# Blocks of 32 tokens in four column tiles, placed inside a big block's second layer

## The chip, the cores and the metric

The kernel runs on one core of a Trainium2 chip. The metric is the device time of that core, in microseconds (us). An execution has a span, from the first to the last instruction that the profile records, and a little time around it that counts too. TensorE multiplies matrices (PE in the profile, PEld for its loads of stationary operands), VectorE (DVE), ScalarE (ACT) and GpSimd (POOL) do the rest, and SyncE (SP) issues transfers.

## The reference: windowed attention, then one expert for each token

Eight sequences of 576 tokens go through attention of 8 heads with a causal window of 64 positions. The result, 4608 rows of 512 numbers, goes into a layer of eight experts:

```
fresh_e = argmax(logits[b, s])
e = fresh_e if s == 0 or local_gate[b, s] < 0.5 else prev_e
p = softmax(logits[b, s])
h = maximum(x[b, s] @ w1[e], 0.0)      # w1[e]: 512 x 1024
out[b, s] = p[e] * (h @ w2[e])         # w2[e]: 1024 x 512
```

So each token uses exactly one expert, and which one is known only after attention. Everything is float32. The numbers of tokens for the experts are uneven, so when an expert's tokens are gathered in blocks, the last of them leave a remainder.

## The kernel before, in words

**Stages.** Attention takes the first 137 us or so. The router (class `Router`) works out for every token its expert, its probability and its place in a list of blocks; `first` does so for the first tokens, `second` for all the rest, beside the first three expert blocks. The result are tables: `idx` (which token stands in which row of which slot of 128 rows), `pw` (its probability), `gx` (the row to gather) and `ej` (the expert of each block). The rest of the time goes to class `Experts`.

**Blocks.** An expert's tokens are cut into big blocks of 256 rows (two slots). A remainder of 65 to 192 takes a small block of 128 rows, one of up to 64 a half block, and more than 192 rounds up to a big block. Since the program is fixed and the numbers are not, `SURE` says how many blocks of each kind are always run: 13 big, 4 small, 4 half, after three big blocks that the first part of the tokens fills (`FB`). If an input needs more, a branch at the end (`more`) runs the others.

**A big block.** Both layers of most big blocks are written as a 2x2 multiplication with seven products in place of eight. The first layer is `big_hidden` (L1164): seven products of 16 records of 128 columns each (L1184), additions on VectorE (L1195) and relus on ScalarE (L1196). It needs sums and differences of quarters of x (`xs`) and w1 (`ws1`), which `prepare` (L1134) has VectorE compute; `big_hidden` itself has VectorE compute those of w2 (`ws2`, L1157) and of the hidden layer (`hs`, L1149). The second layer is `big_result` (L1216): seven products of 8 records of 256 columns each (L1227), copies scaled by the probability on ScalarE (L1232, L1252), three additions on VectorE (L1236), and a scatter of each slot's rows to the output on POOL (L1257). An f32 matmul of the program appears as two records in the profile.

**A half block.** `hidden` (L1275) puts a stationary of 64 columns of w1 into each of two column tiles of TensorE, so that 64 rows of x move through both at once: 64 matmuls, 128 records. `result` (L1294) keeps the hidden layer stationary and moves two halves of w2: 16 matmuls, 32 records. One copy on ScalarE (L1297) and one scatter by half rows (L1298, table `idxh`) follow. A small block uses the same functions with the whole array (L1275, L1307).

**Order.** `run` (L1326) makes a list of blocks. After the three first ones it takes big blocks 0 to 12; after each odd one a half or a small block stands, and one small and one half block come last. For every block in turn it calls `hidden`, then `turn` for the next block (L1123: transposes of the gathered rows on TensorE at L1129, a copy on VectorE at L1130, and `prepare` if the block is big), then `result`. So TensorE's order is hidden layer, transposes of the next block, second layer. From the third block on, the order on TensorE, VectorE and ScalarE is as written; before that only TensorE's is, and a scheduler places the rest.

**Loads.** Each block loads its expert's w1 and w2, 2 MB each, on SP's queue (L1116) into a ring of four buffers, two blocks ahead. A new load waits until the buffer that it takes is free. Rows of x are gathered by an indirect transfer on POOL (L1104). A scatter to the output waits for the landing of the scatter ahead of it.

Of the kernel before, what the change touches and what calls it, by code (L numbers as in the profile page):

```python
# [41 lines left out]
FB = 3  # L42
# [8 lines left out]
NBLK = NB + E + E  # L51
SURE = (LEFT + E * HF) // BIG - E // 2, E // 2, E // 2
# [27 lines left out]
def kernel(  # L80
# [25 lines left out]
                pwh=const.tile([P, E], F32, name="pwh"), idx1=const.tile([P, FIRST], U32, name="idx1"),  # L106
# [585 lines left out]
class Router:  # L692
# [217 lines left out]
    def experts_of(self, ej, n, ends):  # L910

        vec, tl = self.nc.vector, self.tl
        ec = tl("ec", 1, NBLK, E)
        b = 0
        for m, end in ends:
            vec.tensor_tensor(ec[:, b:b + m], self.iob[:, :m].to_broadcast([1, m, E]),
                              self.mid(end[0:1, :]).to_broadcast([1, m, E]), op=Alu.is_ge)
            b += m
        ef = tl("ef", 1, NBLK)
        vec.tensor_reduce(ef[:, :n], ec[:, :n], axis=AX.X, op=Alu.add)  # L920
        vec.tensor_scalar(ej, ef[:, :n], float(E - 1), None, Alu.min)
# [77 lines left out]
    def second(self, psum):  # L999
# [18 lines left out]
        ns = tl("ns", P, E)  # L1018
        self.shifted(ns, rest, HF - 1, P.bit_length() - 1)
        send = tl("send", P, E)  # L1020
        vec.tensor_tensor_scan(send, ns, self.zero[:, :E], 0.0, Alu.add, Alu.add)
        soff = tl("soff", P, E)
        vec.tensor_tensor(soff, send, ns, op=Alu.subtract)
# [3 lines left out]
        nh = tl("nh", P, E)  # L1027
        vec.tensor_tensor(nh, cnt, limh, op=Alu.is_gt)
        hend = tl("hend", P, E)
        vec.tensor_tensor_scan(hend, nh, self.zero[:, :E], 0.0, Alu.add, Alu.add)  # L1030
        hoff = tl("hoff", P, E)
        vec.tensor_tensor(hoff, hend, nh, op=Alu.subtract)
# [9 lines left out]
        vec.tensor_scalar(steph, steph, float(P), float((HF0 - SM0) * P), Alu.mult, Alu.add)  # L1042
        CE = [P, CV, E]
# [5 lines left out]
        yield 6.0, False  # L1049
        plh = tl("plh", *CE)  # L1050
        vec.tensor_tensor(plh, self.rank, mid(limh).to_broadcast(CE), op=Alu.is_ge)
        vec.tensor_tensor(plh, plh, mid(steph).to_broadcast(CE), op=Alu.mult)
        vec.tensor_tensor(pl, pl, plh, op=Alu.add)
# [5 lines left out]
        self.experts_of(ej[:, :NBLK], NBLK, [(NB, bend), (E, send), (E, hend)])  # L1059
        more = tl("more", 1, 1)  # L1060
        vec.tensor_scalar(more, hend[0:1, E - 1:], float(SURE[2]), None, Alu.is_gt)
        vec.scalar_tensor_tensor(more, send[0:1, E - 1:], float(SURE[1]), more, Alu.is_gt, Alu.max)
        vec.scalar_tensor_tensor(ej[:, NBLK:], bend[0:1, E - 1:], float(SURE[0]), more, Alu.is_gt, Alu.max)
        yield 6.0, False
        at = yield from self.table(psum, slice(0, CV), NS, lo, hi, tabs["idx"], tabs["pw"], tabs["gx"])

        for i in range(2):
            vec.tensor_scalar(tabs["idxh"][i * HF:(i + 1) * HF], at[:HF, HF0:], 2.0, float(i), Alu.mult, Alu.add)
            vec.tensor_copy(tabs["pwh"][i * HF:(i + 1) * HF], tabs["pw"][:HF, HF0:])

# [7 lines left out]
class Experts:  # L1078
# [12 lines left out]
    def rows(self, st, n):  # L1091
        tabs = self.tabs
        if n < 0:
            idx, pw, gx, rows = tabs["idx1"], tabs["pw1"], tabs["gx1"], ZR + 1
            slots = range(-2 - 2 * n, -2 * n)
        else:
            idx, pw, gx, rows = tabs["idx"], tabs["pw"], tabs["gx"], N + 2
            slots = range(2 * n, 2 * n + 2) if n < NB else range(SM0 + n - NB, SM0 + n - NB + 1)
        st.update(x=[], slots=slots, idx=idx, pw=pw, rows=P, big=len(slots) == 2, fast=len(slots) == 2 and n not in PLAIN)
        if n >= NB + E:  # L1100
            st.update(half=n - NB - E, rows=HF)
# [21 lines left out]
    def turn(self, st, quiet):  # L1123
        nc, n = self.nc, st["rows"]
        st["xt"] = xt = self.xtp.tile([P, DK, BIG], F32, name="xt")
        for i, x in enumerate(st["x"]):
            tp = self.ps_t.tile([P, DK, P], F32, name="tp")
            for kk in range(DK):
                nc.tensor.transpose(tp[:, kk, :n], x[:n, kk * P:(kk + 1) * P], self.ident[:n, :n])  # L1129
            (nc.scalar.copy if quiet else nc.vector.tensor_copy)(xt[:, :, i * P:i * P + n], tp[:, :, :n])  # L1130
        if st["fast"] and not quiet:
# [84 lines left out]
    def big_result(self, st):  # L1216

        nc = self.nc
        a, s, b, t = st["ha"], st["hs"], st["w2q"], st["w2t"]
# [19 lines left out]
        u = keep(0, px, pw[0])  # L1239
        product(py, s[0], t[0], stop=False)  # L1240
        z = keep(1, py, pw[1])
        product(px, s[1], t[1], False, False)
        v = keep(2, px, pw[0])
        product(pz, a[0][1], b[1][0])
        put(0, 0, pz, u)
        product(px, s[2], t[2], False, False)
        put(1, 1, px, z)
        product(py, s[3], b[1][1], False)
        put(0, 1, py, v)
        self.scatter(st, 0, y[0])  # L1250
        product(px, a[1][1], t[3], False)
        nc.scalar.activation(y[1][:, :w], px, Act.Copy, scale=pw[1])  # L1252
        self.scatter(st, 1, y[1])

# [29 lines left out]
    def result(self, st, step):  # L1284
        nc = self.nc
        if st["fast"]:
            return self.big_result(st)
# [38 lines left out]
    def run(self, ctx, rt, last=None):  # L1326
# [27 lines left out]
        small = list(range(NB, NB + SURE[1]))  # L1354
        half = list(range(NB + E, NB + E + SURE[2]))
        between = half[1:] + small
# [4 lines left out]
        order += between + half[:1]  # L1361
# [3 lines left out]
        for i, n in enumerate(order):  # L1365
# [11 lines left out]
            if i + 2 > FB and i + 2 < len(order):  # L1377
                jobs.append(self.fetch(order[i + 2]))
            self.hidden(jobs[i], quiet, step)
            if i + 1 < len(order):  # L1380
                self.turn(jobs[i + 1], i + 1 < FB)
            self.result(jobs[i], step)

    def more(self, ctx):

        self.space(ctx)
        for n in [*range(SURE[0], NB), *range(NB + SURE[1], NB + E), *range(NB + E + SURE[2], NBLK)]:
# [3 lines left out]
            self.result(st, lambda: None)  # L1391

# [48 lines left out]
```

## Time and profile before

| what | value |
|---|---|
| median of 3 runs | 658.93 us (657.99 to 662.63) |
| the profiled execution | 659.11 us, span 657.1 us |
| TensorE busy | 629.8 us, 96% |
| loads of stationary operands busy | 544.8 us, 83% |
| VectorE busy | 401.2 us, 61% |
| ScalarE, POOL busy | 181.8 us (28%), 125.8 us (19%) |
| records of half blocks: hidden / second layer | 512 of L1275 / 128 of L1294 |
| mean DMA rate | 252 GB/s |

A busy time is the union of an engine's recorded spans; a matmul's span includes its way through the pipeline, so the distance from one start to the next says more of its cost than its own duration. In a timeline a line gives the start (us from the beginning of the span), the duration of the merged group, engine, source line, operation, output and inputs, the tile of TensorE (rows x columns of the stationary operand, written 128*64), the moving shape, and the number of records; square brackets hold the idle time before it and what ended it. Idle time of an engine that is not the bottleneck costs nothing by itself.

### The profile page before, as it was taken

The page shows a single profiled execution, that of the slowest core. Times are in us where ns is not written, and L with a number is a line of the kernel's source. Part 1 is how long each engine was busy: PE and PEld are TensorE (multiplying, and loading weights), DVE is VectorE, ACT ScalarE, POOL GpSimd, SP SyncE. Part 2 cuts the span into 40 slices and gives each one's busy share as a digit, 9 for nine tenths or more (in the row PEclk, how much of TensorE's full clock was granted, in tenths as well). Part 3 has the DMA queues.
Part 4 walks back from the last instruction along what each step waited for, and adds up shares of the span by engine and source line. Part 5 has one row for each costly group of instructions (what it writes and reads, how often), then busy time and mean ns, then how long its engine had stood idle before and what let it go on. Part 6 is the DMA issues. An engine that isn't in the chain of part 4 may idle for free. (4 is left out here: it accounts for less than half of the span.)

```text
span 657.1 us, 14909 instructions
## 1 busy us (share of the span) xinstructions
PE 629.8 (96%) x6431; PEld 544.8 (83%) x6431; DVE 401.2 (61%) x723; ACT 181.8 (28%) x314; POOL 125.8 (19%) x131
## 2 busy tenths in 40 slices
PE   7888988899999999999999999999999999999995
PEld 7777767675757999889989998999799979997974
DVE  6675589665984866378628835852765276527310
ACT  4756655421111232112212121221122112211200
POOL 4322122220014111121104113211311130101011
PEclk9999998899999999999999999999999999999999
DMA  8999999895436555595578748746864685457540
GB/s 337 415 346 360 351 377 355 327 378 199 161 144 241 195 212 218 173 397 204 184 278 315 269 180 314 289 169 215 305 240 165 221 309 219 161 213 283 193 157 23
DMA packets 22032, 165.80 MB, mean 252 GB/s; under 512 B 3485, under 2 KB 4515, under 8 KB 11972
## 3 DMA queue, kind: packets, MB, share of 16 engines
q1 hardware_dynamic: 13108, 135.24, 55.4%
q0 software_dynamic: 8848, 29.50, 11.3%
q8 instruction: 53, 0.87, 0.5%
q14 instruction: 23, 0.19, 0.1%
HBM read 145.85 MB, written 19.40 MB: 251 GB/s over the span
## 5 line engine op out<-in xcount | busy, mean ns | idle before, releaser
L1257 POOL DMA_INDIRECT out_dram<-y,idx x36 | 40.9, 1136 | 335.6 <-DVE y L1236 149.2
L1184 PE MATMUL hp<-xs,ws 128*128 128x128 f32 x672 | 79.6, 275 | 0.0
L1184 PEld LDWEIGHTS hp<-xs,ws 128*128 128x128 f32 x672 | 77.3, 192 | 0.0
L1227 PE MATMUL hp<-ws,hs 128*128 128x256 f32 x336 | 77.1, 379 | 0.0
L1275 PE MATMUL hp<-xt,w 128*64 128x64 f32 (+2 forms) x896 | 74.1, 260 | 0.0
L1275 PEld LDWEIGHTS hp<-xt,w 128*64 128x64 f32 (+1 forms) x896 | 68.6, 161 | 5.8 <-issue 2.4
L1227 PEld LDWEIGHTS hp<-ws,hs 128*128 128x128 f32 x336 | 63.8, 190 | 8.7
L1195 DVE TENSOR_TENSOR h<-hp,keep 128x512 f32<-128x512 f32 x42 | 28.8, 690 | 57.3 <-PE hp L1184 57.3
L1104 POOL DMA_INDIRECT xg<-xs,gx x40 | 45.7, 1144 | 72.7 <-PE tp L1129 58.9
L1307 PE MATMUL yp<-w,h 128*128 128x512 f32 x128 | 56.4, 593 | 0.0
L1184 PEld LDWEIGHTS hp<-xt,w 128*128 128x128 f32 x448 | 53.0, 192 | 2.9 <-issue 1.9
L1184 PE MATMUL hp<-xt,w 128*128 128x128 f32 x448 | 54.9, 276 | 0.0
L1236 DVE SCALAR_TENSOR_TENSOR y<-hp,pw,kept 128x256 f32<-128x256 f32 x42 | 19.7, 480 | 57.1 <-issue 33.3
L1227 PE MATMUL hp<-w,h 128*128 128x256 f32 x224 | 53.3, 381 | 0.0
L416 DVE TENSOR_TENSOR p<-p,mask 128x1024 f32<-128x1024 f32 x31 | 38.6, 1244 | 20.6 <-ACT p L411 20.5
L380 PEld LDWEIGHTS sp<-w 64*64 64x64 f32 x1296 | 37.6, 134 | 16.3 <-issue 13.1
L411 ACT ACTIVATE p<-sp 128x512 f32<-128x512 f32 x72 | 39.3, 596 | 40.1 <-PE sp L380 37.9
L426 PE MATMUL xo<-va,p 128*64 128x74 f32 (+1 forms) x576 | 45.7, 233 | 3.3 <-DVE va L343 3.3
L426 PE MATMUL xo<-vb,p 128*64 128x74 f32 (+1 forms) x576 | 45.7, 233 | 3.2 <-ACT p L300 1.5
L380 PE MATMUL sp<-w 64*64 64x128 f32 (+1 forms) x1296 | 43.3, 265 | 5.5 <-issue 4.7
L426 PEld LDWEIGHTS xo<-vb,p 128*64 128x64 f32 x576 | 39.9, 141 | 7.9 <-issue 4.7
L1307 PEld LDWEIGHTS yp<-w,h 128*128 128x128 f32 x128 | 23.7, 190 | 26.9 <-issue 26.1
(257 smaller groups left out, 945.9 us busy)
## 6 DMA issues: line engine op xcount, KB each, us to landing
w<-in_w_dram SPq DMA_DIRECT2D x48, 2048.0 KB, 9.0
w<-in_kq_dram SPq DMA_DIRECT2D x17, 1024.0 KB, 9.4
xs<-x POOLq DMA_DIRECT2D x9, 1024.0 KB
va<-in_v_dram SPq DMA_DIRECT2D x5, 1184.0 KB
vtt<-in_vt_dram SPq DMA_DIRECT2D x5, 1024.0 KB
va<-in_v_dram SPq DMA_DIRECT2D x3, 1040.0 KB, 9.0
va<-in_v_dram SPq DMA_DIRECT2D x2, 520.0 KB, 6.6
w<-in_kq_dram SPq DMA_DIRECT2D x2, 512.0 KB
```

The costliest lines, as they stand in the source:

```text
L380: nc.tensor.matmul(sp[j][c * WIN:(c + 1) * WIN, a:b], lhsT=kt[h, hp, block * WIN:(block + 1) * WIN], rhs=qt[h, hp, a:b], start=not biased, ...
L411: nc.scalar.activation(p[:, j], sp[j], Act.Exp, scale=DH ** -0.5)
L416: masked.append(nc.vector.tensor_tensor(p, p, m.to_broadcast([P, 2, SC]), op=Alu.mult))
L426: nc.tensor.matmul(xo[par * WIN:(par + 1) * WIN, j, s * VW:s * VW + n], lhsT=p[:, j, b * WIN:(b + 1) * WIN], rhs=w[:, s, 2 * hp + j, :n], ...
L1104: self.nc.gpsimd.indirect_dma_start(out=x, out_offset=None, in_=self.xs[:rows, :], in_offset=bass.IndirectOffsetOnAxis(ap=gx[:, s:s + 1], ...
L1184: nc.tensor.matmul(out[:, m, :], lhsT=a[:, kk, m * P:(m + 1) * P], rhs=b[:, kk, :], start=start and m + kk == 0, stop=stop and (m, kk) == ...
L1195: nc.vector.tensor_tensor(o, x, y, op=add)
L1227: nc.tensor.matmul(out, lhsT=a[:, m, :], rhs=b[:, m, :], start=start and m == 0, stop=stop and m == FK // 2 - 1, skip_group_check=True)
L1236: nc.vector.scalar_tensor_tensor(y[i][:, j * w:(j + 1) * w], x, pw[i], y2, Alu.mult, Alu.add)
L1257: self.nc.gpsimd.indirect_dma_start(out=self.out[:, :], out_offset=bass.IndirectOffsetOnAxis(ap=st["idx"][:, s:s + 1], axis=0), in_=y, in_ ...
L1275: nc.tensor.matmul(hp[a, i, :], lhsT=st["w1"][:, kk, m * P:(m + 1) * P][:, a], rhs=st["xt"][:, kk, :n], start=(kk == 0), stop=(kk == DK - 1))
L1307: nc.tensor.matmul(yp, lhsT=st["h"][:, m, i * P:(i + 1) * P], rhs=st["w2"][:, m, :], start=(m == 0), stop=(m == FK - 1))
```

## The change

A fourth kind of block is added. A remainder is now rounded up to a multiple of 32 and written as 128, 64 and 32 (`count` in `second`): a remainder of up to 32 takes a *quarter* block, 33 to 64 a half, 65 to 96 a half and a quarter, 97 to 192 starts with a small one. Fixed numbers are 13 big, 4 small, 2 half, 2 quarter. A quarter shares a slot of 128 rows with a half of the same number: rows 0 to 63 are the half's, rows 64 to 95 the quarter's. Tables `idxq` and `pwq` serve its scatter by quarter rows.

A quarter's computation comes in three parts, `one`, `turned` and `two`. `one` keeps 32 rows of x stationary in each of four column tiles and moves a fourth of w1's columns through each; the hidden layer comes out with its rows as partitions, so `turned` transposes it; `two` keeps it stationary and moves fourths of w2. These parts are not a block of their own in the order: `big_result` of the big block ahead gets `hooks` and calls one after each of its products: `one` after the first, `turned` after the second, `two` after the third, nothing after the fourth, the transposes and copies of the following block's x after the fifth, its `prepare` after the sixth. Elsewhere the following block is turned and prepared before the second layer, as it was.

Quarters stand after big blocks 2 and 6; small blocks move up to stand after big blocks 1, 3, 5 and 7, one half after 9, and the other half block is last, behind big block 12. In `experts_of` the table of comparisons becomes bf16.

```diff
-NBLK = NB + E + E
-SURE = (LEFT + E * HF) // BIG - E // 2, E // 2, E // 2
+QR = P // 4
+KINDS = NB, NB + E, NB + 2 * E
+NBLK = KINDS[-1] + E
+SURE = (LEFT + E * HF) // BIG - E // 2, E // 2, E // 4, E // 4
...
-        ns = tl("ns", P, E)
-        self.shifted(ns, rest, HF - 1, P.bit_length() - 1)
-        send = tl("send", P, E)
-        vec.tensor_tensor_scan(send, ns, self.zero[:, :E], 0.0, Alu.add, Alu.add)
-        soff = tl("soff", P, E)
-        vec.tensor_tensor(soff, send, ns, op=Alu.subtract)
+        r = tl("r", P, E)
+        self.shifted(r, rest, QR - 1, QR.bit_length() - 1)
+
+        def count(name, x, many):
+
+            n = tl("n" + name, P, E)
+            vec.tensor_scalar(n, x, float(many), None, Alu.is_ge)
+            end = tl(name + "end", P, E)
+            vec.tensor_tensor_scan(end, n, self.zero[:, :E], 0.0, Alu.add, Alu.add)
+            off = tl(name + "off", P, E)
+            vec.tensor_tensor(off, end, n, op=Alu.subtract)
+            return n, end, off
+
+        ns, send, soff = count("s", r, 4)
+        vec.scalar_tensor_tensor(r, ns, -4.0, r, Alu.mult, Alu.add)
+        nh, hend, hoff = count("h", r, 2)
+        vec.scalar_tensor_tensor(r, nh, -2.0, r, Alu.mult, Alu.add)
+        _, qend, qoff = count("q", r, 1)
...
+        vec.tensor_tensor(plh, self.rank, mid(limq).to_broadcast(CE), op=Alu.is_ge)
+        vec.tensor_tensor(plh, plh, mid(stepq).to_broadcast(CE), op=Alu.mult)
+        vec.tensor_tensor(pl, pl, plh, op=Alu.add)
...
-    def turn(self, st, quiet):
+    def turn(self, st, quiet, later=False):
         nc, n = self.nc, st["rows"]
+        a = slice(HF, HF + n) if "quarter" in st else slice(n)
...
-        if st["fast"] and not quiet:
+        if st["fast"] and not quiet and not later:
             self.prepare(st)
...
         product(px, a[0][0], b[0][0], stop=False)
         u = keep(0, px, pw[0])
+        hook()
         product(py, s[0], t[0], stop=False)
         z = keep(1, py, pw[1])
+        hook()
...
+    def quarter(self, st):
+
+        nc, s = self.nc, st["quarter"]
+        w, n = F // 4, D // 4
+
+        def one():
+            yp = self.ps_y.tile([P, D], F32, name="yp")[:, :w]
+            for kk in range(DK):
+                for j in range(4):
+                    nc.tensor.matmul(yp[j * QR:(j + 1) * QR], lhsT=st["xt"][:, kk, :QR],
+                                     rhs=st["w1"][:, kk, j * w:(j + 1) * w], start=kk == 0, stop=kk == DK - 1)
+            st["hq"] = hq = self.one.tile([P, w], F32, name="qh")
+            nc.scalar.activation(hq, yp, Act.Relu)
+
+        def turned():
+            tp = self.ps_t.tile([P, DK, P], F32, name="tp")[:, :w // P]
+            for i in range(w // P):
+                nc.tensor.transpose(tp[:, i], st["hq"][:, i * P:(i + 1) * P], self.ident)
+            st["ht"] = ht = self.one.tile([P, w // P, P], F32, name="qt")
+            nc.scalar.copy(ht, tp)
+
+        def two():
+            yp = self.ps_y.tile([P, D], F32, name="yp")[:, :n]
+            for m in range(FK):
+                for j in range(4):
+                    k, i = divmod(m, w // P)
+                    nc.tensor.matmul(yp[j * QR:(j + 1) * QR], lhsT=st["ht"][:, i, k * QR:(k + 1) * QR],
+                                     rhs=st["w2"][:, m, j * n:(j + 1) * n], start=m == 0, stop=m == FK - 1)
+            y = self.one.tile([P, n], F32, name="qy")
+            nc.scalar.activation(y, yp, Act.Copy, scale=self.tabs["pwq"][:, s:s + 1])
+            nc.gpsimd.indirect_dma_start(
+                out=self.out.rearrange("n (i d) -> (n i) d", i=4),
+                out_offset=bass.IndirectOffsetOnAxis(ap=self.tabs["idxq"][:, s:s + 1], axis=0),
+                in_=y, in_offset=None, bounds_check=4 * N - 1, oob_is_err=False)
+
+        return one, turned, two
...
-        small = list(range(NB, NB + SURE[1]))
-        half = list(range(NB + E, NB + E + SURE[2]))
-        between = half[1:] + small
+        between = [*range(NB, NB + SURE[1]), *range(KINDS[1] + 1, KINDS[1] + SURE[2])]
+        quarters = list(range(KINDS[2], KINDS[2] + SURE[3]))
         for n in range(SURE[0]):
             order.append(n)
             if n % 2 and between:
                 order.append(between.pop(0))
-        order += between + half[:1]
+            elif n % 4 == 2 and quarters:
+                order.append(quarters.pop(0))
+        order += between
+        order.append(KINDS[1])
...
+            if n >= KINDS[2]:
+                continue
             self.hidden(jobs[i], quiet, step)
-            if i + 1 < len(order):
-                self.turn(jobs[i + 1], i + 1 < FB)
-            self.result(jobs[i], step)
+            if i + 1 == len(order):
+                self.result(jobs[i], step)
+                continue
+            self.turn(jobs[i + 1], i + 1 < FB)
+            hooks = ()
+            if order[i + 1] >= KINDS[2]:
+                one, turned, two = self.quarter(jobs[i + 1])
+                after = jobs[i + 2]
+                hooks = one, turned, two, (lambda: None), (lambda: self.turn(after, False, True)), \
+                    (lambda: self.prepare(after))
+            self.result(jobs[i], step, hooks)
```

## The prediction

> **What bounds the kernel now.** First the page: busy time of each engine, then the forty slices.
>
> ```profile
> PE 629.8 (96%) x6431; PEld 544.8 (83%) x6431; DVE 401.2 (61%) x723; ACT 181.8 (28%) x314; POOL 125.8 (19%) x131
> PE   7888988899999999999999999999999999999995
> ```
>
> From slice 8 (131 us) to the last, TensorE is full. So the expert stage is a queue of matmuls, and an edit there is worth the TensorE time it takes out, less any new gap. Next the timeline of TensorE over one big block (313.39), one half block (338.66) and the next big block (347.17).
>
> ```profile
> 313.39 1.95 PE L1184 MATMUL hp<-xt,w 128*128 128x128 f32 x16
> ...
> 325.99 0.46 PE L1129 MATMUL tp<-ident,xg 64*128 64x64 f32 x4
> 326.37 1.99 PE L1227 MATMUL hp<-w,h 128*128 128x256 f32 x8
> ...
> 338.66 3.95 PE L1275 MATMUL hp<-xt,w 128*64 128x64 f32 x128
> ...
> 343.56 3.67 PE L1294 MATMUL yp<-w,h 128*64 128x256 f32 x32
> 347.17 2.05 PE L1184 MATMUL hp<-xt,w 128*128 128x128 f32 x16
> ...
> 372.74 1.95 PE L1184 MATMUL hp<-xt,w 128*128 128x128 f32 x16
> ```
>
> Nothing idles between the groups. A big block followed by a big one lasts 372.74 - 347.17 = 25.57 us; big and half together last 347.17 - 313.39 = 33.78. A half block costs 33.78 - 25.57 = 8.21 us.
>
> Two more stretches of that timeline price packing: the gate's eight matmuls (L312, stationaries of 32 columns in four column tiles), and attention scores (L380) in tiles of 64x64.
>
> ```profile
> 108.84 1.06 PE L312 MATMUL r<-vtt,wg2s 128*32 128x512 f32 x8
> 109.84 1.12 PE L380 MATMUL sp<-w 64*64 64x128 f32 x36
> 110.89 0.66 PE L327 MATMUL r<-ident,gs 128*128 128x128 f32 x4
> ```
>
> Last, the timelines (start, duration, and in brackets the idle time before and its releaser) of VectorE and of the scatters on POOL.
>
> ```profile
> 183.70 0.42 DVE L1157 TENSOR_TENSOR xs<-xt 128x256 f32<-128x256 f32 x1 [3.18 <-ACT xt L1130]
> ...
> 285.21 0.43 DVE L1157 TENSOR_TENSOR xs<-xt 128x256 f32<-128x256 f32 x1
> ...
> 291.38 1.21 DVE L1157 TENSOR_TENSOR ws<-w 128x1024 f32<-128x1024 f32 x1
> ...
> 328.23 0.42 DVE L1130 COPY xt<-tp 128x256 f32<-128x256 f32 x1
> ```
>
> ```profile
> 627.10 0.98 POOL L1257 DMA_INDIRECT out_dram<-y,idx  x1 [21.65 <-DVE y L1236]
> 635.64 0.98 POOL L1257 DMA_INDIRECT out_dram<-y,idx  x1 [7.56 <-DMA out_dram<-y,idx]
> ...
> 651.08 0.98 POOL L1298 DMA_INDIRECT out_dram<-y,idxh  x1 [5.31 <-ACT y L1297]
> ```
>
> A big block's preparation takes VectorE 285.21 to 291.38 = 6.17 us; the sums of w2 then 4.67 (to 296.05), where the first relu addition follows at once: VectorE was behind there already.
>
> **What the Trainium skill says.** "TensorEngine Tiling (Array Packing)", Tiling Modes and Key Properties: 128x32 is four tiles that work in parallel, and changing the mode drains TensorE. The trace agrees: a 512-wide matmul on the whole array takes 7.03/16 = 0.43 us (L1307), so eight in four tiles would be 0.86, and they took 109.84 - 108.84 = 1.00; I read 0.14 as the drain, and L1294 shows as much (3.61 us against 32 x 0.108 = 3.46). "TensorE: Matmul & The Clock Gate", "Wait — 56ns, not 53.3ns?": matmuls never start closer than about 25 ns. Here L380 gives 1.05/36 = 29 ns with the drain, L1275 3.88/128 = 30. "DMA: Bandwidth & Descriptors", Issuing engines are not separate DMA queues: all queues share 16 engines. Agreed: the scatter of 627.10, beside a load of weights, lets the next go after 8.5 us.
>
> **The change part by part.**
>
> *Which blocks.* From the reference's router and the split rules I worked out each expert's leftover. Before: 13 big, 4 small, 4 half. After: 13, 4, 2 half, 2 quarter (leftovers of 9 and 18 tokens). All four counts equal what SURE provides for, so the rare path is not taken. Two half blocks become two quarters; jobs, loads of 4 MB and the 40 scatters stay in number.
>
> *Removed.* 2 x 8.21 = 16.42 us of TensorE.
>
> *Added on TensorE, for a quarter.* Counts are records: an f32 matmul appears as two in the trace. (a) Four transposes of x: the half's take 0.57 us with the switches (338.66 - 313.39 = 25.27 for the big block with them; 25.57 less the 0.87 of eight 128-wide ones = 24.70 without any); I take 0.5 (0.4 to 0.6). (b) `one`: 32 matmuls 256 wide; a whole-array one takes 1.73/8 = 0.216, in four tiles 32 x 0.216/4 = 1.73, with the drain 1.87. (c) `turned`: two transposes, 2 x 0.11 = 0.22, no change of mode. (d) `two`: 64 matmuls 128 wide; 7.14/64 = 0.112 each, over four 0.028, at the start-to-start floor; 64 x 0.028 = 1.79, at 30 ns 1.92; with the drain 2.0. Sum 4.6 us. Bounds: 4.2 with no drains; if only two of four tiles overlapped, (b) 3.5 and (d) 3.6, sum 7.8; not below 4.2, since the columns must stream.
>
> *Added waits on TensorE.* (e) `one` needs the quarter's xt, copied by VectorE after the four `hs` sums. At 328.23 that copy starts 1.86 us after the first product (326.37); I take 0.28 us for 128 elements (0.42 for 256, 0.68 for 512). So xt is ready near 2.2, and `one` could start at 1.8: 0.4 us of gap (0 to 0.5). The other six products queue behind it. (f) The next big block's `prepare` moves from ahead of the second layer's additions to behind the third one. Let T be the end of the sixth product. The addition starts 0.27 after its product and makes room after 0.43, at T + 0.7; prepare ends at T + 6.9; w2's sums at T + 11.5; two relu additions of 0.69 end at T + 12.9. TensorE runs product seven (1.73) and six first-layer products (1.787 each), and asks at T + 12.45 for the second of those additions, since the seventh product accumulates on what it reads. Gap 0.5 us (0 to 1.0). Queued behind it are the block's remaining products. The first sum of w1 comes at T + 3.4, wanted at T + 3.5: 0.1 more. So a quarter costs 4.6 + 0.4 + 0.5 + 0.1 = 5.6 us.
>
> *Hidden.* ScalarE's two copies and the scaling (0.47 us each by L1297's kind) lie under products of 1.73 us; without that cover up to 0.5 each. Weights: the following block's w1 is asked for when the second layer starts (R) and is wanted by VectorE near R + 17; its w2 takes the quarter's freed w1 slot near R + 4 and is wanted near R + 23. A load takes 8.5 us in the median, 10.3 at most: cover of 6 us or more; past it each microsecond is one of TensorE. On POOL the quarter's scatter stands ahead of two gathers and the big block's scatters; the gathers run two blocks ahead, and y buffers are wanted again 20 us later. On SP the order stays.
>
> *Router.* By the order in which the changed program's instructions stand, 15 more on VectorE before the table: three of 296 elements at 0.38 us cadence, 12 small ones at 0.1 to 0.2, some 2.3 to 2.9 us. They fall into the idle 3.18 us ahead of 183.70 (a wait for ScalarE's copy, set by TensorE). I take 0.1 (0 to 0.4). Eight index instructions after the table come behind what the gathers need: 0.
>
> *End.* The last half block now follows a big block, not a small one. With its weights long loaded, scatters don't wait 8.5 us as at 627.10, so the stretch of 657.1 - 650.25 = 6.85 after TensorE stays: 0 (to +1).
>
> *Sum.* -16.42 + 2 x 5.6 + 0.1 = -5.1; I take off the likelihood that (e) and (f) partly overlap with drains already counted (0.3): -5.4. The profiled execution took 659.11 (span 657.1 and 2.0 around it), 0.2 over the median of 658.93. So 659.11 - 5.4 = 653.7.
>
> **The rivals.** *The waits vanish* (0.15): VectorE is in time, a quarter costs 4.4 to 4.6; -16.4 + 9.0 = -7.4: 651.7. For it: the gaps are tenths, within what adjacent instructions overlap. Against: 328.23 shows the copy late by itself. *Packing or waits worse than shown* (0.17): `one` and `two` at a third more (+1.2), or gaps doubled (+1.0): quarter 6.8, gain 2.8, 656.3; at two-tile pace 660.5. For it: `two` lies at the issue floor and loads a new stationary for each 28 ns. Against: L312. *Slower* (0.05): the four column tiles don't overlap at all in `one` and `two`, because they share one stationary's rows: 32 x 0.216 + 64 x 0.112 = 14.1 us in place of 3.9; the quarter costs 15.8, twice 7.6 more than a half: 674. It decides once packing gains less than 14.1/(3.9 + 2.6) = 2.2-fold. Against: L1294 shares a stationary in two tiles and reaches 1.9. *It doesn't do what it says* (0.02): a count beyond SURE runs the branch of leftovers; each block there at least its own load of 8.5 us, so above 680. The nearest leftover (165) is 5 tokens from a limit.
>
> **How the numbers follow.** The sum has 0.61; its own range is 652.3 to 655.5. For 8 in 10, I leave 4 in 100 below 651.2 and the top of the worse case, slower and branch above 657.8. One per cent, 6.6 us, is about what a measurement of this kernel can tell from no change; the forecast lies inside it. Faster by over 1% (under 652.3): most of the first rival and the sum's edge, 0.17. Slower (above 665.5): 0.07. Within: 0.76.
>
> **What would show it.** In the profile after: no L1275-like groups but for two half blocks; in two big blocks' second layers a group 128*32 of 32 matmuls lasting about 1.9 us and one of 64 about 2.0; a gap of 0.4 ahead of the first, waiting for VectorE's xt; a gap near 0.5 before the following block's seventh first-layer product, waiting for VectorE's addition; some 30.7 us from the start of that big block to the start of the next. If the groups take 3.5 each, packing was wrong; if VectorE waits for a DMA at the sums of w1 or w2, the cover of weights was; a flag transpose waiting over 2 us near 202 would be the router.

## The result

The changed kernel takes 654.55 us (median of 12 runs, 650.78 to 656.88), the kernel before 658.92 in the same group: -4.4 us, ratio 0.9925 (95% interval 0.9905 to 0.9946). Forecast were 653.7 and a range of 651.2 to 657.8. Two later groups, each on one chip with both kernels, gave 653.08 against 657.60 (0.9936, 0.9913 to 0.9959) and 651.80 against 656.95 (0.9924, 0.9895 to 0.9952). So the gain is 4.4 to 5.2 us, below one per cent, and none of the three intervals reaches 1. The profiled execution of the changed kernel took 656.34 us, span 654.3.

The page of the changed kernel, busy times and TensorE's forty slices:

```profile
PE 625.4 (96%) x6307; PEld 538.5 (82%) x6307; DVE 402.2 (61%) x742; ACT 182.6 (28%) x318; POOL 124.4 (19%) x131
PE   8889887999999999999999999999999999999996
```

TensorE is as full as before. Its timeline over a big block with a quarter inside (297.28 to 327.97) and into the block behind it:

```profile
297.28 1.95 PE L1212 MATMUL hp<-xt,w 128*128 128x128 f32 x16
...
308.00 1.95 PE L1212 MATMUL hp<-xs,w 128*128 128x128 f32 x16
309.88 0.43 PE L1157 MATMUL tp<-ident,xg 32*128 32x32 f32 x4
310.24 1.99 PE L1260 MATMUL hp<-w,h 128*128 128x256 f32 x8
312.46 1.93 PE L1303 MATMUL yp<-w,xt 128*32 128x256 f32 x32 [0.23 <-DVE xt L1158]
314.33 1.99 PE L1260 MATMUL hp<-ws,hs 128*128 128x256 f32 x8
316.16 0.38 PE L1311 MATMUL tp<-ident,qh 128*128 128x128 f32 x2
316.38 1.89 PE L1260 MATMUL hp<-ws,hs 128*128 128x256 f32 x8
318.20 1.95 PE L1320 MATMUL yp<-w,qt 128*32 128x128 f32 x64
320.08 1.99 PE L1260 MATMUL hp<-w,h 128*128 128x256 f32 x8
...
327.97 1.95 PE L1212 MATMUL hp<-xt,w 128*128 128x128 f32 x16
...
336.90 1.95 PE L1212 MATMUL hp<-xt,ws 128*128 128x128 f32 x16
339.05 2.05 PE L1212 MATMUL hp<-xs,w 128*128 128x128 f32 x16 [0.20 <-DVE h L1223]
```

A big block alone lasted 25.57 us before; this one lasts 327.97 - 297.28 = 30.69. `one` takes 314.33 - 312.46 = 1.87, `turned` 0.22, `two` 1.88. Two gaps name the releasers that the prediction named: VectorE's copy of xt ahead of `one`, VectorE's relu addition ahead of the following block's seventh first-layer product. VectorE's timeline shows why:

```profile
184.87 0.55 DVE L942 TENSOR_TENSOR one<-ios,hi 128x378 bf16<-128x378 f32 x1
186.38 0.43 DVE L1185 TENSOR_TENSOR xs<-xt 128x256 f32<-128x256 f32 x1 [0.95 <-ACT xt L1158]
...
312.13 0.28 DVE L1158 COPY xt<-tp 128x128 f32<-128x128 f32 x1
...
336.58 1.22 DVE L1185 TENSOR_TENSOR ws<-w,ws 128x1024 f32<-128x1024 f32 x1
337.71 1.88 DVE L1223 TENSOR_TENSOR h<-hp,keep 128x512 f32<-128x512 f32 x3
```

xt is ready at 312.41, 0.05 before `one` starts. The last sum of w2 and three relu additions follow each other without a pause: VectorE is late there. In the router the idle 3.18 us has shrunk to 0.95, so the added instructions used 2.23 of it; in the other profiles of this kernel 0.98 is left.

To divide the difference, take the expert stage: from the first product of the first big block after the flags (202.42 in the kernel before) to the end of the last matmul. Start, length, and the rest to the end of the span, all from the timelines of TensorE:

| kernel | start | length | rest |
|---|---|---|---|
| before | 202.42 | 447.83 | 6.85 |
| changed, three profiles | 205.10 / 201.61 / 200.28 | 442.66 / 441.40 / 441.39 | 6.52 / 7.11 / 7.60 |
| before, with the changed order of blocks | 200.83 | 446.87 | 8.93 |
| loops exchanged | 202.28 | 454.72 | 6.44 |
| tiles in pairs | 201.70 | 445.84 | 7.67 |
| quarter on its own | 201.62 | 441.98 | 6.45 |
| no quarter work | 203.14 | 432.07 | 14.97 |
| scatter only | 202.08 | 432.12 | 7.27 |
| five more router instructions | 202.16 | 443.03 | 6.71 |
| both waits moved | 200.82 | 445.83 | 7.55 |
| sums split | 202.21 | 439.87 | 6.46 |

The stage became 6.4 us shorter (447.83 to 441.40). The first profile is 1.26 longer, mostly by one pause of 1.00 us at 213.47 that the others don't have. Its late start, 205.10, is no part of the change either: the later two start at 201.61 and 200.28. One source of such scatter stands at the start of attention, in the kernel before and then in the changed kernel's first profile:

```profile
5.33 1.46 PE L380 MATMUL sp<-w 64*64 64x128 f32 x38
7.32 1.11 PE L380 MATMUL sp<-w 64*64 64x128 f32 x34 [0.54 <-ACT p L411]
```

```profile
5.33 2.39 PE L383 MATMUL sp<-w 64*64 64x128 f32 x38
8.05 1.98 PE L383 MATMUL sp<-w 64*64 64x128 f32 x34 [0.33 <-ACT p L414]
```

The same instructions take up to 1.8 times as long. The Trainium skill, "TensorE: Matmul & The Clock Gate", What's actually happening, says that TensorE starts at half clock and is released after a busy window of about 3.4 us that runs free of the kernel, so that the moment varies. The trace's clock entries agree that it varies: full clock begins at 5.7 us in the kernel before and at 11.8, 6.1 and 7.2 in the three profiles of the changed one.

But the expert stage does not inherit this delay as it is. Three places of attention in the changed kernel's first profile, then two of them in its second:

```profile
58.59 0.27 PE L429 MATMUL xo<-vb,p 128*64 128x65 f32 x1 [0.82 <-ACT p L303]
...
78.55 0.55 PE L383 MATMUL sp<-w 64*64 64x128 f32 x8 [1.82 <-issue]
...
87.14 0.39 PE L804 MATMUL r<-ident,vk 128*14 128x128 f32 x2 [0.67 <-DVE va L346]
```

```profile
57.99 0.27 PE L429 MATMUL xo<-vb,p 128*64 128x65 f32 x1 [0.82 <-ACT p L303]
...
83.29 0.39 PE L804 MATMUL r<-ident,vk 128*14 128x128 f32 x2 [0.66 <-DVE va L346]
```

The first profile is only 0.60 us behind at 58 us; it is 3.85 behind at 87, after a pause of 1.82 and 3.4 us at half clock from 80.05. The version with both waits moved, below, gets full clock only at 12.0, and its stage starts at 200.82. So the scatter arises all through attention, and part of it is made up again. The start of the stage in a single profile is uncertain by some 5 us (200.28 to 205.10 for one kernel), and only its length is compared here.

### The profile page after: what moved, and what is told of

Its sections match the earlier page's. It is cut to its first block, busy times and chain, and to the rows that moved or that the text cites. A ratio compares the mean times of both kernels' runs of the same rounds, so it can differ in the third digit from the quotient of the medians.

```text
span 654.3 us, 14680 instructions
## 1 busy us (share of the span) xinstructions
PE 625.4 (96%) x6307; PEld 538.5 (82%) x6307; DVE 402.2 (61%) x742; ACT 182.6 (28%) x318; POOL 124.4 (19%) x131
## 5 line engine op out<-in xcount | busy, mean ns | idle before, releaser
L1351 PE MATMUL hp<-xt,w 128*64 128x64 f32 (+2 forms) x640 | 65.9, 275 | 0.0
L1351 PEld LDWEIGHTS hp<-xt,w 128*128 128x128 f32 (+1 forms) x640 | 60.8, 170 | 4.6 <-issue 1.1
L383 PEld LDWEIGHTS sp<-w 64*64 64x64 f32 x1296 | 38.7, 138 | 14.1 <-issue 10.7
L1260 PEld LDWEIGHTS hp<-w,h 128*128 128x128 f32 x224 | 41.3, 190 | 5.6 <-issue 0.4
```

Of the source, the lines that this page charges most:

```text
L383: nc.tensor.matmul(sp[j][c * WIN:(c + 1) * WIN, a:b], lhsT=kt[h, hp, block * WIN:(block + 1) * WIN], rhs=qt[h, hp, a:b], start=not biased, ...
L1260: nc.tensor.matmul(out, lhsT=a[:, m, :], rhs=b[:, m, :], start=start and m == 0, stop=stop and m == FK // 2 - 1, skip_group_check=True)
L1351: nc.tensor.matmul(hp[a, i, :], lhsT=st["w1"][:, kk, m * P:(m + 1) * P][:, a], rhs=st["xt"][:, kk, :n], start=(kk == 0), stop=(kk == DK - 1))
```

## The experiments

**Loops exchanged.** Each column tile goes through its whole contraction before the next one.

```diff
-            for kk in range(DK):
-                for j in range(4):
+            for j in range(4):
+                for kk in range(DK):
...
-            for m in range(FK):
-                for j in range(4):
+            for j in range(4):
+                for m in range(FK):
```

> The two loops of each product of a quarter are exchanged: all 16 products of one column tile come before those of the next, so neighbours never lie in different tiles except at three borders. Theory, that a quarter is cheap because its four column tiles work at the same time: the first layer takes 32 x 0.216 = 6.9 us, the second 64 x 0.112 = 7.2, a quarter 10.3 us more, the time near 654.5 + 20.6 = 675 us. Rival, that the cost is set by columns of the array or by rows moved whatever the order: within 1 us of the changed kernel, 654.5.

665.86 us, ratio 1.0125 (1.0089 to 1.0161). TensorE's timeline:

```profile
308.38 4.59 PE L1303 MATMUL yp<-w,xt 128*32 128x256 f32 x32 [0.23 <-DVE xt L1158]
312.91 2.00 PE L1260 MATMUL hp<-ws,hs 128*128 128x256 f32 x8
...
316.78 5.96 PE L1320 MATMUL yp<-w,qt 128*32 128x128 f32 x64
322.66 1.99 PE L1260 MATMUL hp<-w,h 128*128 128x256 f32 x8
```

`one` takes 4.53 us and `two` 5.88, in place of 1.87 and 1.88. The rival falls. The theory has the cause right but not the size: 10.4 us, not 14.1. The starts of single records in that trace tell why (us; tile by count, eight records each):

```
tile 0:  308.382  308.622  308.838  309.054  309.270  309.486  309.701  309.917
tile 1:                                      309.276  309.516  309.731  309.947 ...
```

Inside a tile a record starts 0.216 after the one before, the full price of 256 columns. But tile 1 starts 6 ns after tile 0's fifth record, while three of tile 0 still stand in line. I read this as a line per tile in which three records can wait behind the running one; TensorE takes instructions in order until such a line is full. Then each border saves four slots: `one` takes 4 + 4 + 4 + 8 = 20 slots of 0.216 and 0.14 for the change of mode, 4.46 (measured 4.53); `two` 12 + 12 + 12 + 16 = 52 of 0.109 and 0.14, 5.81 (5.88). In the kernel as changed four starts follow each other by 6.6 ns and the next round comes 0.216 or 0.109 later: 8 x 0.216 + 0.14 = 1.87 and 16 x 0.109 + 0.14 = 1.88, as measured.

**Tiles in pairs.** Tiles 0 and 1 in turn, then 2 and 3.

```diff
-            for kk in range(DK):
-                for j in range(4):
+            for j, kk in ((j + i, kk) for j in (0, 2) for kk in range(DK) for i in range(2)):
+                if True:
...
-            for m in range(FK):
-                for j in range(4):
+            for j, m in ((j + i, m) for j in (0, 2) for m in range(FK) for i in range(2)):
+                if True:
```

> The two products of a quarter go through the column tiles in two pairs: all of tiles 0 and 1, in turn, then all of tiles 2 and 3. Theory, by single starts in the version with exchanged loops (a tile starts a new 256-wide record every 216 ns and a 128-wide one every 109, other tiles start beside it, and some four records of the next tile come forward at a border): the first layer takes 16 x 0.216 = 3.5 us less up to 0.4 for the border, the second 32 x 0.109 = 3.5 less up to 0.3, so a quarter costs 2.5 to 3.2 us more. Rival, that the order doesn't matter as long as neighbours lie in different tiles: 1.9 us each, as in the changed kernel.

657.26 us in one run. TensorE's timeline:

```profile
307.80 2.82 PE L1303 MATMUL yp<-w,xt 128*32 128x256 f32 x32 [0.23 <-DVE xt L1158]
310.55 1.99 PE L1260 MATMUL hp<-ws,hs 128*128 128x256 f32 x8
...
314.42 3.29 PE L1320 MATMUL yp<-w,qt 128*32 128x128 f32 x64
317.64 1.99 PE L1260 MATMUL hp<-w,h 128*128 128x256 f32 x8
```

2.75 and 3.22 us: a quarter costs 2.2 more, and the stage is 2 x 2.2 = 4.4 longer. The rival falls. I had given the border too little (0.4 and 0.3); with four slots it is (4 + 8) x 0.216 + 0.14 = 2.73 and (12 + 16) x 0.109 + 0.14 = 3.19. So the line of three waiting records fits all six durations. The number three was chosen to fit, and that it is a queue in hardware is inferred from starts alone.

**No quarter work.** The hooks for `one`, `turned` and `two` are empty.

```diff
-                hooks = one, turned, two, (lambda: None), (lambda: self.turn(after, False, True)), \
+                hooks = (lambda: None), (lambda: None), (lambda: None), (lambda: None), (lambda: self.turn(after, False, True)), \
```

> Leaves out the computing of the two quarter blocks (first layer, transposition, second layer, scaling and scatter; the rows of those 27 tokens are not written); their gather, weights, transposes of x and the late preparation of the following block stay. Theory, by the changed kernel's own timeline: a quarter's parts take 1.87 + 0.22 + 1.88 us of TensorE and a wait of 0.4 ahead of them, 4.4 us; two are 8.7, so some 9 us less than the changed kernel, near 646 us, and the block with the quarter lasts about 26.3 us in place of 30.7. The wait ahead of the following block's seventh first-layer product stays (0.3 to 0.4 us), since VectorE's preparation is as late as before. Rival, that the parts partly lie in time that TensorE would lose anyway: 4 us less or fewer, near 650.

653.26 us, ratio 0.9941 (0.9919 to 0.9963): by the time, the rival. But the stage in the table is 9.3 us shorter than the changed kernel's 441.40, and the saving is lost behind it, where the rest is 14.97 us. The instructions of the program's end, POOL's queue (count, then shortest/median/longest in ns):

```profile
L1531 POOLq DRAIN  x3: 46/103/7502, 641.8 to 649.9; - x3
```

In the changed kernel the longest is 805 ns. So this time says nothing on the quarter's cost; hence the next run.

**Scatter only.** As above, but the scatter stays; the matmuls of `two` are taken out, and it writes scaled rows of the unit matrix.

```diff
...
-            nc.scalar.activation(y, yp, Act.Copy, scale=self.tabs["pwq"][:, s:s + 1])
+            nc.scalar.activation(y, self.ident, Act.Copy, scale=self.tabs["pwq"][:, s:s + 1])
...
-                hooks = one, turned, two, (lambda: None), (lambda: self.turn(after, False, True)), \
+                hooks = (lambda: None), (lambda: None), two, (lambda: None), (lambda: self.turn(after, False, True)), \
```

> Leaves out the first layer, the transposition and the second layer of the two quarters, but keeps their scatter: the rows of those 27 tokens get scaled rows of the unit matrix. Theory: what made the version without any quarter work only 1.3 us faster was the end, where POOL's last drain took 7.50 us in place of 0.81; with the scatter kept the drain is 0.8 again and the time 8 to 9.5 us under the changed kernel's in the same group, near 645. Rival, that TensorE's saving is given back wherever TensorE ends early: the drain is 7 us again and the time within 2 us of the changed kernel's.

642.77 us, 10.3 under the changed kernel in that group (0.9769, 0.974 to 0.9798, to the kernel before), with a stage 9.3 shorter. The end is ordinary again:

```profile
L1525 POOLq DRAIN  x3: 46/103/805, 639.8 to 641.2; - x3
```

A quarter's work costs 9.3/2 = 4.6 us of TensorE, paid in full; nothing of it lay in time lost anyway. Why two scatters fewer lengthened POOL's last drain stays open.

**Order alone.** The kernel before with the changed order: small blocks behind big blocks 1, 3, 5 and 7, half blocks behind 2, 6 and 9 and at the end.

```diff
-        between = half[1:] + small
+        between = small + half[1:2]
+        late = half[2:]
...
+            elif n % 4 == 2 and late:
+                order.append(late.pop(0))
```

> The kernel before with the changed kernel's order of blocks: small blocks after big blocks 1, 3, 5 and 7, half blocks where the changed kernel has its quarters and its half, and a half block last, behind a big one. Theory, that the gain is the work of the two blocks and not their order: the same as the kernel before within 1 us, 658 to 660. Rival, that standing behind a big block or the changed end gave part of it: 656 to 657 or less.

659.01 against 657.15 us, ratio 1.002 (1.0005 to 1.0036): no gain in time, if anything a loss of 0.2%. The stage is 0.96 shorter, of which 0.35 is a pause at 213.72 that the profile of before had and this one has not; the rest behind the stage is 2.1 longer. POOL's last scatter:

```profile
650.72 0.98 POOL L1298 DMA_INDIRECT out_dram<-y,idxh  x1 [4.29 <-issue]
```

It starts 2.5 us after ScalarE's y (647.75 + 0.47), and the profile shows no releaser; in the three profiles of the changed kernel that distance is 0.29 to 0.66. What holds it is open. For the sum this run gives the fairer base: 446.87 to 441.40 is -5.47 for the two quarters themselves.

**Quarter on its own.** After the big block's second layer, without hooks.

```diff
             if n >= KINDS[2]:
+                self.turn(jobs[i + 1], False)
+                for part in self.quarter(jobs[i]):
+                    part()
                 continue
...
-            if order[i + 1] >= KINDS[2]:
-                one, turned, two = self.quarter(jobs[i + 1])
...
```

> The quarter runs as a block of its own after the big block's second layer; the following block is turned and prepared ahead of it. Theory, that lying inside the second layer covers ScalarE's steps: TensorE waits about 0.6 to 1 us for the relu before the transposes and as long for the copy after them; the waits of 0.4 ahead of the first part and of 0.4 ahead of the seventh product go; a quarter costs 0.5 to 1.5 us more, the time is 655.5 to 657.5 us. Rival, that the place is worth nothing (the waits exchanged are equal): 654.5. Second rival, that the second layer's weights land too late for a quarter that stands alone: a wait for a DMA of several us, above 660.

652.04 us, ratio 0.9927 (0.9902 to 0.9952), what the changed kernel reaches. TensorE's timeline:

```profile
318.65 1.93 PE L1303 MATMUL yp<-w,xt 128*32 128x256 f32 x32
321.09 0.44 PE L1311 MATMUL tp<-ident,qh 128*128 128x128 f32 x2 [0.51 <-ACT qh L1306]
321.99 1.95 PE L1320 MATMUL yp<-w,qt 128*32 128x128 f32 x64 [0.46 <-ACT qt L1313]
```

The waits for ScalarE appear as expected, with no wait for a DMA; in return the two waits for VectorE go. The stage is 0.58 us longer, 0.3 per quarter. The place inside the second layer is worth that by single profiles; in the time the first rival, that the place is worth nothing, can't be told from it. The theory's 0.5 to 1.5 was too much because it took ScalarE's two waits for 1.2 to 2.0 us together: they are 0.51 + 0.46 = 0.97, and the two waits that go cost 0.75 (from the split sums below).

**Five more router instructions.**

```diff
         vec.tensor_tensor(plh, plh, mid(stepq).to_broadcast(CE), op=Alu.mult)
+        for _ in range(5):
+            vec.tensor_scalar(plh, plh, 1.0, None, Alu.mult)
```

> Five more multiplications by 1.0 of the same 296 elements in the router's chain on VectorE, 0.4 us each, 2 us together. Theory, that the changed kernel's 2.2 us of router work was hidden in VectorE's idle 3.18 us, of which 0.95 are left: the idle stretch ahead of the x sums near 186 us shrinks to zero and the chain's end is 1 us later than in the changed kernel; TensorE waits for the flag about as long as before (1.3 us), and what it waits for comes later only if the tail of attention no longer covers it. Rival, that the router was on the path already: the start of the expert stage is later by 2 us or more.

653.62 us in one run. The chain grew by 1.67 us (the next addition starts at 169.60, in the second profile of the changed kernel at 167.93), the idle stretch ahead of the x sums is gone, and TensorE waits 1.92 us for the flag in place of 1.32:

```profile
202.05 0.27 PE L159 MATMUL r<-ident,ok 128*1 128x128 f32 x1 [1.92 <-DVE t L956]
202.16 3.44 PE L1214 MATMUL hp<-xt,w 128*128 128x128 f32 x16
```

So 0.98 was free and the remaining 0.7 arrived as 0.6. More came behind it: the first product takes 3.24 us in place of 1.86. A stretch (length, busy us of PE, PEld, DVE, ACT, POOL, then granted clock, DMA share, GB/s):

```profile
202.50:205.90 3.40, 3.40 (x19) 3.40 (x18) 2.33 (x19) 0.26 (x1) 1.96 (x2) 0.50 0.94 358
```

For 3.4 us after the wait the clock is at half, which costs 1.7: the stage is 1.63 longer than 441.40.

**Both waits moved.** The parts start one product later, and behind a quarter all four sums of w2 move behind the second relu addition.

```diff
-            st["w2t"] = self.right("ws2", w2)
+        if not st.get("behind"):
+            st["w2t"] = self.right("ws2", w2)
...
         relu(hq[1][1], px, z)
+        if st.get("behind"):
+            st["w2t"] = self.right("ws2", w2)
...
-                hooks = one, turned, two, (lambda: None), (lambda: self.turn(after, False, True)), \
+                after["behind"] = True
+                hooks = (lambda: None), one, turned, two, (lambda: self.turn(after, False, True)), \
```

> The parts of a quarter move one product later (the first after the second product instead of the first), and after a quarter VectorE's sums of w2 stand behind the second relu addition. Theory: both waits of TensorE go, 0.4 and 0.36 us per quarter; the big block with the quarter lasts 30.3, the following one 25.1; 1.5 us less than the changed kernel in the same group. Rival, that the waits only move (the block of x is wanted later, but the sums of w2 now come too late for the second layer): no difference, within 0.5 us, with a new wait on VectorE's sums at the second layer.

655.18 us, 2.1 more than the changed kernel in that group (0.9965, 0.9949 to 0.9981, to the kernel before). Both waits are gone and a new one stands in the second layer of the block behind; the rival has the place, though not the size. TensorE's timeline, and then a stretch as above:

```profile
338.89 5.38 PE L1263 MATMUL hp<-ws,hs 128*128 128x256 f32 x16 [1.94 <-DVE hs L1177]
344.11 1.89 PE L1263 MATMUL hp<-w,h 128*128 128x256 f32 x8
...
478.37 3.69 PE L1263 MATMUL hp<-ws,hs 128*128 128x256 f32 x16 [1.86 <-DVE hs L1177]
```

```profile
339.70:343.10 3.40, 3.40 (x10) 2.69 (x9) 1.58 (x3) 0.47 (x1) 0.00 (x0) 0.50 0.70 294
```

The sums of w2 now keep the sums of h late. After the first of the two waits the clock is at half again (5.22 us between starts for 3.46), after the second not. In this profile the stage is 4.43 us longer than 441.40; the 18 runs spread from 652.61 to 658.45, and their median is only 2.1 higher.

**Sums split.** As the last, but two sums of w2 before the relu additions and two behind the second one; `differences` computes those of the four sums that it is told to.

```diff
...
-        st["w2t"] = self.right("ws2", w2)
+        st["w2t"] = ws2 = self.sums("ws2", w2)
+        behind = st.get("behind")
+        self.differences(ws2, w2, (0, 1) if behind else (0, 1, 2, 3))
...
         relu(hq[1][1], px, z)
+        if behind:
+            self.differences(ws2, w2, (2, 3))
...
```

> As in the version with both waits removed, the parts of a quarter come one product later; but of the four sums of w2 that follow a quarter only the last two stand behind the second relu addition, the first two ahead of the first one. Theory, from the idle stretches of VectorE in the last two profiles: 2.3 us lie free ahead of the first addition (two sums of 1.14 need 2.3) and 2.8 us between the second addition and the sums of h (two sums and the third addition need 3.0), so neither wait returns and the new one of 1.9 us for the sums of h is gone or at most 0.2: a big block with a quarter lasts 30.4 us, the block behind it 25.1, the time is 1.0 to 1.5 us less than the changed kernel's in the same group. Rival, that the order on VectorE can't be had without a wait somewhere: within 0.5 us of the changed kernel.

> The changed kernel unaltered, for comparison in the same group: 4 to 5 us faster than the kernel before.

650.89 us (0.9913, 0.9887 to 0.9938, to the kernel before), the changed kernel beside it 651.80. VectorE's timeline behind the quarter:

```profile
329.84 1.23 DVE L1190 TENSOR_TENSOR ws<-w,ws 128x1024 f32<-128x1024 f32 x1
330.98 0.68 DVE L1229 TENSOR_TENSOR h<-hp,keep 128x512 f32<-128x512 f32 x1
332.72 0.69 DVE L1229 TENSOR_TENSOR h<-hp,keep 128x512 f32<-128x512 f32 x1 [1.06 <-PE hp L1218]
333.33 1.21 DVE L1190 TENSOR_TENSOR ws<-w 128x1024 f32<-128x1024 f32 x1
334.46 1.22 DVE L1190 TENSOR_TENSOR ws<-w,ws 128x1024 f32<-128x1024 f32 x1
```

VectorE waits for TensorE at the second addition: it is early again. TensorE has no gap in either block, which last 30.39 and 25.03 us; in the third profile of the changed kernel they last 30.69 and 25.48. So the two waits together cost 0.30 + 0.45 per quarter, and the stage is 1.52 shorter. The medians differ by 0.9, with intervals that overlap; the stage shows the gain, the time alone could not. Of the versions that compute everything this one has the shortest stage and the lowest median.

**The changed kernel again**, beside the versions with scatter only and with both waits moved.

> The changed kernel unaltered, beside the kernel before and the variants of this group. Theory: 4 to 5 us faster than the kernel before, ratio 0.9925 to 0.994, and its span divides as in the first profile: a big block with a quarter inside lasts 30.7 us, and what lies ahead of the expert stage varies by 2 to 3 us between executions. Rival, that the stage ahead of the experts became longer by the 2.7 us that the first profile showed: its start at 205 us again.

653.08 us, with a start of 201.61: the rival falls, as told above.

## Why the prediction was right

The cost of a quarter was 5.6 us in the prediction and is 5.12 in its own big block and 0.45 in the next, 5.57. By its steps:

- *(a)* predicted 0.5: 0.36 and 0.09 ahead of it (309.88 - 308.00 = 1.88 for a product of 1.79), 0.45.
- *(b)* 1.87, measured 1.87. *(c)* 0.22, measured 0.22.
- *(d)* 2.0, measured 1.88. The price was near, its reason wrong. I took 28 to 30 ns between starts as a floor that binds here; starts in different tiles lie 6.6 ns apart, and what binds is 0.109 us for 128 columns in each tile. The floor of about 25 ns that the prediction cites does not hold between tiles in this trace, and the trace of before could have told: the eight records of L312, which the prediction uses to price packing, start in two rounds of four, 6.6 ns apart. Nearer is what the Trainium skill gives in "TensorE: Matmul & The Clock Gate", Part 3, Measured speedup vs the span model: about 4 ns of issue for each further tile.
- *(e)* 0.4: the gap is 0.39 (312.46 - 310.24 - 1.83), and taking it away brought 0.30. *(f)* 0.5: the gap is 0.36, taking it away brought 0.45. The 0.1 for the first sum of w1 does not appear.
- Left out of the sum: each return to the whole array costs the next product 0.10 (316.16 - 314.33 = 1.83 for 1.73), three times 0.3. It fills the place of what (a), (d), (f) and the sum of w1 had too much. 0.45 + 1.87 + 0.22 + 1.88 + 0.39 + 0.30 = 5.11 accounts for the 5.12. That 5.6 meets 5.57 so closely is luck: the parts were near, and their errors cancel.

*Removed* stands: 16.42 less 2 x 5.57 is 5.28, and the stage became 5.47 shorter against the same order of blocks. The 0.3 taken off for overlap has no counterpart that I can point to; it was rather luck that it covers the missing 0.2. The other 0.96 of the stage's 6.4 us came with the order, and is no gain in the time of that kernel.

*Router*: 2.3 to 2.9 us were predicted into 3.18; 2.23 went in, and the flag's wait stayed at 1.32 in all three profiles. The run with five more shows that this cover was nearly used up. What the bf16 table in `experts_of` does to that chain was not run on its own. *Hidden*: VectorE has no wait at the sums of w1 and w2 behind a quarter, so weights came in time; without the cover of the second layer ScalarE's copies leave TensorE idle for 0.51 and 0.46 us. *End*: 6.5 to 7.6 us against 6.85, about the predicted 0 to +1.

Of the rivals, *the waits vanish* was not what happened. The split sums make both waits vanish and gain 6.1 us in their group (650.89 against 656.95), where the rival had 7.2 (658.9 to 651.7): what remains of a quarter is 5.57 - 0.75 = 4.8 us, not its 4.4 to 4.6. *Packing at two-tile pace*, priced at 1.6 us more for each product, costs 0.88 and 1.34 in the run with tiles in pairs. *Slower* comes about in another order of the loops, though not for the reason given there, a shared stationary: with neighbours in the same tile the two products take 10.4 us (14.1 in the rival) and the kernel is 8.7 us slower than before. What decided the sign of this change is that the loop over column tiles is the inner one.

The forecast of 653.7 was 0.9 below the first median and 0.6 and 1.9 above the other two. Of the 2.75 us between these medians 1.97 are shared by the kernel before (658.92, 657.60 and 656.95 in the same groups); what sets them is open. As a gain, 5.2 us were forecast from the median of before, and 4.4, 4.5 and 5.2 measured. The prediction took one per cent for about what a measurement can tell from no change; these intervals tell 0.75% from it.

## What to carry to other kernels

Packing into column tiles pays in full only if consecutive matmuls go to different tiles: here the order of two loops alone was worth 13 us of the stage. An engine off the critical path needs its order looked at in both directions: moving all four sums to remove a wait of 0.4 made one of 1.9, moving two removed both. Compare a stage of the trace, from its first to its last instruction, when the gain sought is smaller than the scatter of the time; and when work is left out to price it, look at the end of the program before believing the total.

## What the hardware showed unexpectedly

- A column tile takes a new f32 record of 256 columns every 0.216 us and one of 128 every 0.109; other tiles start 6 to 7 ns later, past up to three records that wait for a busy tile.
- POOL's last drain took 7.50 us in the program with two scatters fewer, 0.81 in the others looked at.
- Full and half clock change on a grid. In each of the thirteen profiles all changes of the clock lie whole multiples of 3.413 us after the first one. Cut on that grid, TensorE's idle time tells when the clock falls: ahead of the last matmul it fell fifteen times, always at the end of a window in which TensorE had been idle for 1.82 to 3.18 us in all; one window with 1.86 brought no fall, and none with 1.7 or less did. So idle time within a window fits, and the length of a wait does not; where between 1.8 and 1.9 us the limit lies stays open. The wait of 1.92 us in the run with five more router instructions lies inside one window, and half clock followed. A pause of 3.30 us in the changed kernel's first profile (102.29 to 105.59) is cut in two by a border and cost no clock; nor did the waits of 1.3 us for the flag in the other twelve profiles. The two cases in stretches as above:

```profile
199.08:202.49 3.41, 1.49 (x14) 1.08 (x12) 3.38 (x8) 0.00 (x0) 1.03 (x1) 1.00 1.01 303
```

```profile
100.53:103.94 3.41, 1.76 (x52) 1.46 (x48) 3.31 (x13) 1.51 (x4) 2.39 (x2) 1.00 0.98 349
103.94:107.35 3.41, 1.76 (x52) 1.60 (x56) 2.91 (x13) 1.76 (x2) 0.43 (x1) 1.00 1.01 428
```

The Trainium skill, "TensorE: Matmul & The Clock Gate", HAM oscillation — how this bites in real kernels, warns of idle gaps over about 3.4 us; here waits of two were enough. With TensorE full afterwards such a fall cost 1.63 us (the router run's stage) and 1.76 us (5.22 - 3.46, both waits moved) more than the wait itself.
